# A heavier weight for the 47-point groups in the pace that mixes spectral steps into channel mixing

## The chip, the core and the metric

The kernel runs on one core of one Trainium2 chip. The metric is device microseconds of one execution, lower is better; what is compared is the median of several runs. A profiled execution has its own time, and inside it a span from the first to the last instruction.

## The reference

The input `x` is 8 batches of 3008 positions by 256 channels in float32. Two blocks follow one another.

```python
X = np.fft.rfft(x, axis=1)
Yr = Xr @ w_r - Xi @ w_i + b_r          # complex 256x256 mixing of channels
Yi = Xr @ w_i + Xi @ w_r + b_i
Yr = sign(Yr) * max(|Yr| - 0.01, 0)     # the same for Yi
x = np.fft.irfft(Yr + 1j * Yi, n=3008, axis=1)

h = max(x.T @ w_tok1, 0) @ w_tok2       # token mixing, 3008 -> 256 -> 3008
u = x + h.T
out = u + max(u @ w_ch1, 0) @ w_ch2     # channel mixing, 256 -> 1536 -> 256
```

## The kernel before

**The arithmetic.** Matrix products that need float32 accuracy are made from a high and a low part of each operand: `mm3` (lines 195 to 198) issues three matmuls, high by high, high by low and low by high. So most products stand in the profile as three groups, at L196, L197 and L198, and each operand costs a cast on ScalarE (L146) or a copy on VectorE (L148), and a subtraction at L149 on VectorE or GpSimd, that make its two parts (`split`).

**The two kinds of work.** The spectral side works on units: batch 0 (unit 0), batch 1 (unit 1), then the pairs of batches 2 and 3, 4 and 5, 6 and 7 (units 2, 3 and 4). For a unit it does two things in turn.

- The 47-point groups (`dft47`, lines 286 to 312, 13 of them per unit). A group loads a tile `x` of up to 480 KB on SyncE's DMA queue (L439), three groups ahead; forms sums and differences (`sum_diff`, tile `sd`: GpSimd adds at L247, VectorE subtracts at L248; for unit 1 VectorE does both); splits them into `xh` (ScalarE, L146) and `xl` (VectorE, L149); multiplies them on TensorE (`stage1`, six matmuls into the PSUM tiles `p`); evicts the products on ScalarE into `a` (L269); and stores `a` to DRAM on ScalarE's DMA queue (L271, tile `a_d`). The pool of `a` has two buffers, so the eviction of one group waits until the store of the group two before it has landed. Units 2, 3 and 4 have two batches: a matmul is 512 columns wide, and tile `a` is 480 KB. Unit 1 has half of that.
- The spectral steps (`spectral`, lines 556 to 599). A step is one of 12 pairs of frequencies for one batch: `forward` (eight small matmuls at L469 into `px`, evicted by ScalarE to `xf` at L471, summed by GpSimd at L472, split to `xth` on ScalarE and `xtl` on VectorE), then one step later `mix` (18 matmuls into `pm`, then bias and soft threshold on VectorE at L498 to L506, and a split `yh`, `yl` on ScalarE and GpSimd), then three or four steps later, once for all batches of the unit, `inverse` (`pi`, stored to DRAM as `b_d`) and `tokens` (`gp`).

The channel side (`channel`, lines 800 to 881) handles a chunk of up to 512 positions: 12 times `first` (six matmuls into `ph`; ScalarE makes `hh` at L814, VectorE makes `hlo` at L815) and `second` (six matmuls into `po`). Now and then it builds the input of the next chunk (`make_u`, tile `pu`), for which tiles `wt` of 940 KB and `b` of 480 KB are loaded on SyncE's queue.

**How the two are put together.** Channel mixing of a unit has spectral work of later units beside it (`BESIDE`, line 40): unit 1 beside the channel mixing of unit 0, unit 2 beside that of unit 1, units 3 and 4 beside that of unit 2. After about 1575 us there is channel mixing alone. `channel` and `spectral` are generators, which give back the TensorE time of what they have just issued, as a planned figure in microseconds: a chunk in pieces of 1.37 or 2.73, a `make_u` as 3.6; a group as 0.7 for one batch and 1.4 for two (line 312), a step as 0.9 for `forward`, 2.15 for `mix`, and per batch 0.68 for `inverse` and 1.37 for `tokens`. Per batch that is 13 times 0.7 and 12 times 5.1, or 70.3 (line 1054).

The loop at the end (lines 1045 to 1077) holds what is left: `left_s` of spectral work and `left_c` of channel work. The pace is `left_s / left_c`, and after each piece of the channel it issues spectral pieces until the two are in proportion again:

```python
while left_s > pace * left_c:
    step = next(sp, None)
    ...
    left_s -= step
```

Spectral work says `"wait"` twice per unit, before its first group (units 2 to 4, line 288) and between the groups and the steps (line 560). Then 10 units of channel work pass alone (`hold`), and the pace is worked out anew from what is left. Three groups of unit 1 are issued before the loop begins; what they count for is `done`.

The instructions of one engine run in the order of its own queue, which is close to the order of the program but not the same: where the program is built, matmuls of neighbouring pieces are interleaved.

Of the kernel before, what the change touches and what calls it, by code (L numbers as in the profile page):

```python
# [17 lines left out]
B, N, C = 8, 3008, 256  # L18
# [5 lines left out]
UNITS = [[0], [1]] + [[2 * p, 2 * p + 1] for p in range(1, NP)]  # L24
NG = 13
# [11 lines left out]
SEVEN = (3, 4)  # L37
SPILL = (3, 4)
CW7 = 2 * CW
BESIDE = {0: [1], 1: [2], 2: [3, 4]}  # L40


# [84 lines left out]
def tile_kernel(ctx: ExitStack, tc: tile.TileContext, io):  # L127
# [115 lines left out]
    def sum_diff(x, g, w, eng, pool):  # L243
        if eng is None:
            return x
        sd = t4([120, 2, w], "sd") if pool is None else wk.tile([120, 2, w], F32, tag=("xtl", "xf", "wt", "et")[g % 4], name="sd", bufs=2)
        eng.tensor_tensor(out=sd[:, 0], in0=x[:, 0], in1=x[:, 1], op=ALU.add)  # L247
        V.tensor_tensor(out=sd[:, 1], in0=x[:, 0], in1=x[:, 1], op=ALU.subtract)  # L248
        return sd

    def split_x(sd, w):
        xh, xl = hl([120, 2, w], "xh"), hl([120, 2, w], "xl")
        split(xh, xl, sd, S, V)
        return xh, xl

    def stage1(sd, dst, g, w, pool):
        n = GS if g < NG - 1 else N2 - GS * (NG - 1)
        a = ev([120, 2, w], "a") if pool is None else pool.tile([120, 2, w], F32, name="a", bufs=4)
        each = 512 // w
        for i0 in range(0, 2, each):  # L260
            pt = bank("p1")
            for i in range(i0, i0 + each):
                o = (i - i0) * w
                if pool is None:
                    mm3(pt[:, o:o + w], f1r[:, 0, i], f1r[:, 1, i], sd[0][:, i], sd[1][:, i], True, True)
                else:
                    PE.matmul(pt[:120, o:o + w], lhsT=f1[:, i], rhs=sd[:, 0], start=True, stop=False)
                    PE.matmul(pt[:120, o:o + w], lhsT=f1[:, 2 * i], rhs=sd[:, 1], start=False, stop=True)
            S.copy(out=a[:, i0:i0 + each].rearrange("p i w -> p (i w)"), in_=pt[:120])  # L269
        rows = dst.rearrange("(i n) k w -> (n k) i w", i=2)  # L270
        PUT.dma_start(out=rows[g * 120:g * 120 + n * KH, :, :w], in_=a[:n * KH])  # L271


    def stage1_turned(sd, z, g):
        n = GS if g < NG - 1 else N2 - GS * (NG - 1)
        pt = bank("p1")
        for t in range(2):
            for i in range(2):
                o = (2 * t + i) * GS * KH
                PE.matmul(pt[:, o:o + GS * KH], lhsT=sd[:, i, t * 128:(t + 1) * 128], rhs=f1[:, i], start=True, stop=True)  # L280
        S.copy(
            out=z.rearrange("p k (q n) -> p q k n", q=4)[:, :, :, g * GS:g * GS + n],
            in_=pt[:, :4 * GS * KH].rearrange("p (q n k) -> p q k n", q=4, n=GS)[:, :, :, :n],
        )

    def dft47(load, dst, w, ahead, eng, pool=None, turned=False):
        xs = [load(g) for g in range(ahead)]
        yield "wait" if eng is G else 0.0
        sds = {}

        def prepare(g):
            if g < NG:
                sds[g] = sum_diff(xs[g], g, w, eng, pool)
                xs[g] = None

        def divide(g):
            if g < NG and pool is None:
                sds[g] = split_x(sds[g], w)

        prepare(0)  # L300
        prepare(1)
        divide(0)
        for g in range(NG):
            if g + ahead < NG:
                xs.append(load(g + ahead))
            prepare(g + 2)
            divide(g + 1)
            if turned:
                stage1_turned(sds.pop(g), dst, g)
            else:  # L310
                stage1(sds.pop(g), dst, g, w, pool)
            yield 0.7 * w / C

    def f2cols(k1):
        j0 = (15 * k1) % N2
# [11 lines left out]
    def prepare_w1(pool, after):  # L327
        def load(g):
            f = load_wide(None, 2 * DT, pool, ("hl", "o")[g % 7 % 2], raw=raws.pop(g), after=after.get(g)).rearrange("p (i w) -> p i w", i=2)
            load_raw1()  # L330
            return f

        return dft47(load, a_w, DT, 2, None, pool)
# [222 lines left out]
    def spectral(u):  # L556
        p = parts(u)
        nb = p.nb
        yield from dft47(p.load_unit, p.a, p.w, 3, V if u == 1 else G)
        yield "wait"  # L560
        steps = [(kp, b) for kp in range(KP) for b in range(nb)]
# [42 lines left out]
    def begin(sp):  # L604
# [14 lines left out]
        with tc.tile_pool(name="early", bufs=1) as early:  # L619
# [3 lines left out]
            wc["fw"] = early.tile([128, 2, 128], F32, name="fw")  # L623
            z = wc["z"] = const.tile([128, KH, 2 * 128], F32, tag="w1", name="z")
            x = dft47(p.load_unit, z, p.w, NG, V, early, True)
            DMA.dma_start(out=wc["eye"], in_=io["eye"])
            next(x)
# [81 lines left out]
    for u, bs in enumerate(UNITS):  # L709
        total, at = N * len(bs), 0  # L710
        step = CW7 if u in SEVEN else CW
        widths = [k * TOKS for k in sizes] if u == 0 else [total % step] + [step] * (total // step)
# [47 lines left out]
    def make_u(g):  # L760
# [6 lines left out]
        for m in homes:  # L767
            if m not in ufs:
                ufs[m] = wc["uf"].tile([128, 2, CW7 if chunks[m][0] in SEVEN else CW], F32, name="uf", bufs=3)
        for ct in range(2):  # L770
# [230 lines left out]
    def channel7(ns):  # L1001
        channels.close()
        wc["tail"] = ctx.enter_context(tc.tile_pool(name="tail", bufs=1, reuse_waits="tile"))
        behind = None
        half = NF // 2
        for n in ns:
            after = n + 1 if n + 1 < len(chunks) else None
            mine = list(needs[after]) if after else []
            for p in range(half):
                hs = first7(n, p)  # L1010
                if behind:
                    second7(*behind, 0, (0, 1))
                if p < len(mine):
                    make_u(mine[p])
                    if p + 1 < len(mine):
                        load_wt2(mine[p + 1])
                        load_b2(mine[p + 1])
                if p == half - 2:
                    load_ahead(n + 2)
                if behind:  # L1020
                    second7(*behind, 1, (0, 1))
                    if p == 0:
                        for k in range(2):
                            finish7(behind[0], k, 2)
                behind = n, p, hs
                if after and p == half - 2:
                    sum_u(after)
                    for i in range(2):
                        split_u7(after, i)
                if after and p == half - 1:  # L1030
                    for i in range(2, 7):
                        split_u7(after, i)
        for k in range(2):
            for f in range(2):
                second7(*behind, f, (k,))
            finish7(behind[0], k, 2 - k)

    def run(gen):
        for _ in gen:
            pass  # L1040
# [3 lines left out]
    done = begin(sp)  # L1044
    for n, (u, at, cw) in enumerate(chunks):
        if u in SEVEN:
            channel7(range(n, len(chunks)))
            break
        if at == 0:
            if u:  # L1050
                sp, done = chain.from_iterable(spectral(v) for v in BESIDE[u]), 0.0
            else:
                sp = chain(sp, *(spectral(v) for v in BESIDE[u][1:]))
            left_s = sum(len(UNITS[v]) for v in BESIDE[u]) * 70.3 - done
            mine = [w for cu, _, w in chunks if cu == u]
            made = sum(k for gu, _, _, k in groups if gu == u) - sizes[0]
            left_c = 32.7 * (sum(mine) - mine[-1]) / CW + 3.6 * made * TOKS / GW + 0.5
            pace, hold = 0.0, left_c - (25.0 if u == 0 else 0.0)
        for c in channel(n):
            if c == "end":  # L1060
                run(sp)
                left_s = -1e9
                continue
            left_c -= c
            if hold is not None:
                if left_c > hold:
                    continue
                pace, hold = left_s / left_c, None
            while left_s > pace * left_c:
                step = next(sp, None)  # L1070
                if step is None:
                    left_s = -1e9
                elif step == "wait":
                    hold = left_c - 10.0
                    break
                else:
                    left_s -= step
# [36 lines left out]
```

## Time and profile before

| what | value |
|---|---|
| median of 3 runs | 2419.73 us (2414.97 to 2424.8) |
| time of the profiled execution | 2420.43 us |
| its span, first to last instruction | 2418.6 us |
| TensorE busy in the span | 2382.5 us |
| mean granted clock of TensorE in the span | 0.998 |
| channel mixing beside spectral work | about 150 to 1575 us |
| groups of unit 2, 3 and 4 on TensorE | 475 to 523, 846 to 893, 1213 to 1259 us |
| DMA traffic over the span | 250.29 MB, mean 103 GB/s |

Busy time of TensorE counts each matmul from its start to a modelled end, and these overlap; so a busy TensorE may still be a stalled one in part, but an idle one is surely waiting. The rows of a view by windows give a stretch of the span, its length, then for each engine its busy microseconds with the count of instructions, the granted clock of TensorE as a share of full speed, the mean busy share of the 16 DMA engines, and GB/s.

### The profile page before, as it was taken

The page shows a single profiled execution, that of the slowest core. Times are in us where ns is not written, and L with a number is a line of the kernel's source. Part 1 is how long each engine was busy: PE and PEld are TensorE (multiplying, and loading weights), DVE is VectorE, ACT ScalarE, POOL GpSimd, SP SyncE. Part 2 cuts the span into 40 slices and gives each one's busy share as a digit, 9 for nine tenths or more (in the row PEclk, how much of TensorE's full clock was granted, in tenths as well). Part 3 has the DMA queues.
Part 4 walks back from the last instruction along what each step waited for, and adds up shares of the span by engine and source line. Part 5 has one row for each costly group of instructions (what it writes and reads, how often), then busy time and mean ns, then how long its engine had stood idle before and what let it go on. Part 6 is the DMA issues. An engine that isn't in the chain of part 4 may idle for free.

```text
span 2418.6 us, 32117 instructions
## 1 busy us (share of the span) xinstructions
PE 2382.5 (99%) x12632; PEld 2077.9 (86%) x12632; DVE 1324.2 (55%) x2070; ACT 1080.3 (45%) x1931; POOL 307.2 (13%) x259
## 2 busy tenths in 40 slices
PE   8999999989999999999999999999999999999999
PEld 7878999978888878888878888898888889888887
DVE  7985655345444455454555544545555554555554
ACT  6764444243333253333353433345445444544543
POOL 0000222022222122222222222000000000000000
PEclk9999999999999999999999999999999999999999
DMA  8874344362323362323472231422221122222100
GB/s 209 249 221 146 96 123 143 107 200 90 93 89 93 102 210 75 117 79 104 129 226 92 88 97 45 134 72 60 72 64 48 42 66 81 59 72 64 48 1 35
DMA packets 145155, 250.29 MB, mean 103 GB/s; under 512 B 10421, under 2 KB 98317, under 8 KB 145005
## 3 DMA queue, kind: packets, MB, share of 16 engines
q1 hardware_dynamic: 114649, 192.67, 27.0%
q10 hardware_dynamic: 30356, 55.58, 7.1%
q8 instruction: 99, 1.62, 0.3%
q14 instruction: 51, 0.42, 0.1%
HBM read 161.84 MB, written 86.38 MB: 103 GB/s over the span
## 4 chain that ended last, share of the span: by engine, by line
PE 91%; DVE 3%; DMA 3%; ACT 1%; issue 1%; SPq 1%; POOL 0%; ACTq 0%; DVEq 0%; POOLq 0%
PE po L196 10%; PE po L198 10%; PE po L197 10%; PE ph L196 5%; PE ph L197 5%; PE ph L198 5%; PE pu L776 5%; PE px L469 3%; PE pm L196 2%; PE pm L198 2%; PE pm L197 2%; PE sx L196 2%; PE sx L198 2%; PE sx L197 2%; PE pu L196 2%; PE pu L197 2%
## 5 line engine op out<-in xcount | busy, mean ns | idle before, releaser
L196 PE MATMUL po<-hh,w2h 128*128 128x512 f32 (+4 forms) x1176 | 451.8, 384 | 0.0
L197 PE MATMUL po<-hlo,w2h 128*128 128x512 f32 (+4 forms) x1176 | 449.0, 382 | 0.0
L198 PE MATMUL po<-hh,w2l 128*128 128x512 f32 (+4 forms) x1176 | 448.8, 382 | 0.0
L815 DVE SCALAR_TENSOR_TENSOR hlo<-ph,hh 128x512 fp32r<-128x512 f32 (+4 forms) x300 | 196.5, 655 | 253.2 <-ACT hh L814 251.9
L814 ACT ACTIVATE hh<-ph 128x512 fp32r<-128x512 f32 (+4 forms) x300 | 171.7, 573 | 279.8 <-PE ph L198 271.5
L198 PEld LDWEIGHTS po<-hh,w2l 128*128 128x128 f32 x1176 | 221.1, 188 | 38.6
L197 PEld LDWEIGHTS po<-hlo,w2h 128*128 128x128 f32 x1176 | 221.2, 188 | 37.6 <-DVE hlo L815 0.5
L196 PEld LDWEIGHTS po<-hh,w2h 128*128 128x128 f32 x1176 | 221.3, 188 | 37.3
L196 PE MATMUL ph<-uh,w 128*128 128x512 f32 (+4 forms) x600 | 230.7, 385 | 6.3 <-ACT a L269 4.9
L197 PE MATMUL ph<-ul,w 128*128 128x512 f32 (+4 forms) x600 | 227.4, 379 | 0.0
L198 PE MATMUL ph<-uh,w 128*128 128x512 f32 (+4 forms) x600 | 226.8, 378 | 0.0
L944 ACT ACTIVATE hh<-sn 128x512 fp32r<-128x512 f32 (+1 forms) x288 | 180.5, 627 | 57.9 <-DVE sn L964 37.8
L945 DVE SCALAR_TENSOR_TENSOR hlo<-sn,hh 128x512 fp32r<-128x512 f32 (+1 forms) x288 | 193.5, 672 | 7.0 <-ACT hh L944 0.6
L149 DVE TENSOR_TENSOR xtl<-xf,xth 128x768 fp32r<-128x768 f32 x84 | 81.4, 969 | 139.6 <-ACT xth L146 139.6
L953 DVE TENSOR_TENSOR sn<-sq,sn 128x512 f32<-128x512 f32 (+1 forms) x72 | 48.9, 679 | 195.5 <-PE sq L198 181.0
L196 PE MATMUL pm<-wmh,xth 128*128 128x256 f32 x504 | 146.9, 292 | 2.8 <-ACT xth L146 2.8
L198 PE MATMUL pm<-wmh,xtl 128*128 128x256 f32 x504 | 142.3, 284 | 1.0 <-DVE xtl L149 1.0
L949 ACT COPY sn<-sx 128x512 f32<-128x512 f32 (+1 forms) x72 | 41.7, 579 | 227.5 <-PE sx L198 227.4
L197 PE MATMUL pm<-wml,xth 128*128 128x256 f32 x504 | 142.3, 283 | 0.0
L783 ACT COPY uf<-pu 128x470 f32<-128x470 f32 (+20 forms) x164 | 61.3, 407 | 179.2 <-PE pu L776 178.7
L776 PEld LDWEIGHTS pu<-g,b 96*128 96x128 f32 x1024 | 130.8, 191 | 3.4
L196 PEld LDWEIGHTS ph<-uh,w 128*128 128x128 f32 x600 | 113.0, 188 | 23.7 <-ACT a L269 6.4
(185 smaller groups left out, 4858.0 us busy)
## 6 DMA issues: line engine op xcount, KB each, us to landing
wt<-wt_d SPq DMA_DIRECT2D x28, 940.0 KB, 5.7
x<-in_x SPq DMA_DIRECT2D x39, 480.0 KB, 5.0
a<-a_d SPq DMA_DIRECT2D x36, 512.0 KB, 3.8
b_d<-bt ACTq DMA_DIRECT2D x36, 512.0 KB, 3.3
a_d<-a ACTq DMA_DIRECT2D x36, 480.0 KB, 4.7
wt<-wt_d SPq DMA_DIRECT2D x21, 752.0 KB, 4.9
b<-b_d SPq DMA_DIRECT2D x32, 480.0 KB, 6.3
aw<-w_d SPq DMA_DIRECT2D x48, 256.0 KB, 2.7
```

Source lines behind the costliest of these rows:

```text
L149: lo_eng.tensor_tensor(out=lo, in0=src, in1=hi.bitcast(F32), op=ALU.subtract)
L196: PE.matmul(out, lhsT=wh, rhs=xh, start=start, stop=False, skip_group_check=more)
L197: PE.matmul(out, lhsT=wh, rhs=xl, start=False, stop=False, skip_group_check=more)
L198: PE.matmul(out, lhsT=wl, rhs=xh, start=False, stop=stop, skip_group_check=more)
L469: PE.matmul(pt[:, o:o + 128], lhsT=x, rhs=f2cols(2 * kp + ab), start=True, stop=True)
L776: PE.matmul(pt[:, s * TOKS:(s + 1) * TOKS], lhsT=b2[:, s, cs], rhs=g2[:, 0 if s0 + s == 0 else 1], start=False, stop=s == k - 1)
L783: S.copy(out=ufs[m][:, ct, lo - at:hi - at], in_=pt[:, lo - c0:hi - c0])
L814: S.activation(out=hh, in_=pt, func=AF.Relu)
L815: V.scalar_tensor_tensor(out=hlo, in0=pt, scalar=0.0, in1=hh.bitcast(F32), op0=ALU.max, op1=ALU.subtract)
L944: S.activation(out=hh, in_=t, func=AF.Relu)
L945: V.scalar_tensor_tensor(out=hlo, in0=t, scalar=0.0, in1=hh.bitcast(F32), op0=ALU.max, op1=ALU.subtract)
L953: V.tensor_tensor(out=snap[0], in0=q, in1=snap[0], op=ALU.add)
```

## The change

A group beside channel mixing counts for 1.75 per batch in place of 0.7, in the figure that it gives back and in the sum that the pace is worked out from. `NG` is 13. No instruction is added, removed or altered in itself; the order in which the program issues them changes. The groups of the preparation that come with a pool of their own keep 0.7.

```diff
+SLOW = 1.75
 BESIDE = {0: [1], 1: [2], 2: [3, 4]}
...
-            yield 0.7 * w / C
+            yield (SLOW if pool is None else 0.7) * w / C
...
-            left_s = sum(len(UNITS[v]) for v in BESIDE[u]) * 70.3 - done
+            left_s = sum(len(UNITS[v]) * (70.3 + NG * (SLOW - 0.7)) for v in BESIDE[u]) - done
```

## The prediction

> **What bounds the kernel now.** I read the page first, for how much there is to win.
>
> ```profile
> span 2418.6 us, 32117 instructions
> PE 2382.5 (99%) x12632; PEld 2077.9 (86%) x12632; DVE 1324.2 (55%) x2070; ACT 1080.3 (45%) x1931; POOL 307.2 (13%) x259
> ```
>
> TensorE is busy for all but 36.1 us of the span, and the change takes no matmul away. So a gain can come only from those 36 us, and from time in which TensorE runs slowly. The next question is where they lie. I went through the span in windows of 25 us, and then asked for the stages that stood out: the groups of units 2, 3 and 4 (first three rows), those of unit 1 after them, a stretch of steps of units 2, 4 and 3, and channel mixing alone in the last row.
>
> ```profile
> core 0: us, PE busy (x) PEld busy (x) DVE busy (x) ACT busy (x) POOL busy (x), PEclk, DMA share, GB/s
> 475.00:525.00 50.00, 43.73 (x197) 35.99 (x196) 28.93 (x28) 28.54 (x47) 15.63 (x9) 0.93 0.80 239
> 845.00:895.00 50.00, 47.47 (x229) 39.55 (x228) 30.93 (x32) 30.35 (x50) 16.08 (x9) 1.00 0.71 215
> 1213.00:1263.00 50.00, 47.44 (x225) 38.49 (x225) 28.05 (x29) 30.09 (x49) 16.18 (x9) 1.00 0.78 232
> 185.00:210.00 25.00, 25.00 (x144) 22.60 (x143) 21.34 (x43) 16.52 (x31) 0.00 (x0) 1.00 0.67 196
> 575.00:725.00 150.00, 149.88 (x861) 132.22 (x861) 73.06 (x109) 58.98 (x103) 38.01 (x36) 1.00 0.29 91
> 1325.00:1475.00 150.00, 149.51 (x856) 132.04 (x855) 71.13 (x106) 57.83 (x103) 38.07 (x35) 1.00 0.29 91
> 950.00:1100.00 150.00, 149.51 (x848) 131.64 (x848) 67.21 (x100) 56.79 (x99) 33.12 (x31) 1.00 0.31 94
> ...
> 425.00:475.00 50.00, 50.00 (x283) 48.02 (x281) 17.11 (x27) 12.19 (x26) 3.18 (x2) 1.00 0.25 71
> ```
>
> The reader sees two regimes. In the steps TensorE idles 0.12 to 0.49 us in 150. In the groups of the three double units it idles 6.27, 2.53 and 2.56 us in 50, and in the first of them the granted clock is 0.93. In those rows DMA is at 215 to 239 GB/s, where the steps have 91 to 94. Unit 1's groups, half as large, idle nothing at 196 GB/s. Next, who TensorE waits for, over the whole span, and below it what ScalarE waits for between 470 and 530 us.
>
> ```profile
> PE p L197 <- DVE xl L149: 6.2, 7, 1.6
> PE ph L196 <- ACT a L269: 4.9, 3, 2.3
> PE pm L196 <- ACT xth L146: 2.8, 4, 1.1
> PE p L196 <- ACT a L269: 0.5, 1, 0.5
> PE pm L198 <- DVE xtl L149: 1.0, 2, 0.5
> ```
> ```profile
> ACT a L269 <- DMA a_d<-a: 10.7, 4, 5.5
> ```
>
> Columns are microseconds, times, longest. Eleven waits (6.2 + 4.9 + 0.5 us) belong to the groups. Where the releaser is ScalarE's eviction `a`, ScalarE itself stood up to 5.5 us for a store of an earlier group to land, and everything behind it in its queue stood too, the `hh` of channel mixing included. The DMA view of 475 to 525 us shows the crowd (issues, KB each, median us to landing):
>
> ```profile
> a_d<-a ACTq DMA_DIRECT2D x12, 480.0 KB, 5.0
> x<-in_x SPq DMA_DIRECT2D x6, 480.0 KB, 6.1
> wt<-wt_d SPq DMA_DIRECT2D x2, 940.0 KB, 7.7
> b<-b_d SPq DMA_DIRECT2D x2, 480.0 KB, 10.0
> ```
>
> **What the change does to the order.** I ran the loop by hand on its own planned figures. When the groups of unit 2 begin, `left_c` is 163.8 both before and after; `left_s` is 2 x 70.3 = 140.6 before and 2 x (70.3 + 13 x 1.05) = 167.9 after. The pace goes from 0.858 to 1.025. A group of two batches is paid with 1.4 / 0.858 = 1.63 us of channel work before and 3.5 / 1.025 = 3.41 us after; with its own 1.4 us it comes every 3.0 us, then every 4.8. The same for unit 3 (0.736 to 0.879): 3.3, then 5.4. Unit 4 (0.817 to 0.976): 3.1, then 5.0. Unit 1 (0.421 to 0.486, one batch): 2.4, then 4.3. Before, two or three groups of a double unit often stand together between two pieces of channel work; after, 3.5 exceeds what one piece of 2.73 pays for, and they stand singly. The steps pay for it. After their hold, unit 2 has 122.4 us of steps to place beside 129.8 of channel work before and 107.1 after: pace 0.943, then 1.143. Unit 1: 0.456, then 0.529; unit 3: 0.763, then 0.910; unit 4: 0.890, then 1.092. That is 16 to 23% closer. All steps still end before the channel mixing beside them does, so no flush at a unit's end is added, and the 845 us after 1575 us are untouched.
>
> **Groups: what goes.** First, idle time in the three rows: 6.27 + 2.53 + 2.56 = 11.4 us. Second, the clock: 7% of 50 us, 3.5 us. Third, what a wait costs beside its idle time:
>
> ```profile
> 508.66 0.40 PE L197 MATMUL p<-xl,f1r 120*128 120x512 f32 x1
> 508.90 0.39 PE L198 MATMUL p<-xh,f1r 120*128 120x512 f32 x1
> 511.58 0.47 PE L196 MATMUL ph<-uh,w 128*128 128x448 f32 x1 [2.29 <-ACT a L269]
> 511.89 0.36 PE L197 MATMUL ph<-ul,w 128*128 128x448 f32 x1
> ```
>
> In a row the next matmul starts 0.24 us after the one before, though that one lasts 0.40; idle time is counted from its end, so a wait hides 0.16 us more, and the first matmul after it takes 0.47 where its neighbour takes 0.36. That is some 0.25 us for each of ten such waits in these stages (one of the eleven I leave to the preparation): 2.5 us. Together 17.4 us could go.
>
> Would they go? In the 50 us of unit 2, 12 stores, 6 loads of `x`, 2 of `wt` and 2 of `b` were asked for. A unit has 13 stores and those 6 loads, 19 x 0.49 MB = 9.3 MB; beside channel work alone there are 71 GB/s. At one group in 3.0 us, 13 groups take 39 us and ask for 239 + 71 = 310 GB/s, which no window of the table shows; at 4.8, 5.4 and 5.0 us they take 62, 70 and 65 us and ask for 150, 133 and 143, with the 71 some 221, 204 and 214 GB/s. The nearest rows are unit 1 with 196 GB/s and no idle time, and unit 3 with 215 and 5%, which holds pairs and triples that the change takes apart. Each store may take two groups' distance to land, some 6.0 us before and 9.6 after, against a median of 5.0. So I let the even spacing remove most, and keep 2.5 us of waits (between 0, by unit 1's row, and 6, by 5% of 62 and 65 us), where a `wt` and a `b` land in the middle of a group.
>
> The clock term needs a look of its own, in windows of 2 us.
>
> ```profile
> 511.00:513.00 2.00, 1.42 (x6) 1.05 (x6) 0.50 (x2) 2.00 (x4) 0.00 (x0) 0.92 0.24 91
> 513.00:515.00 2.00, 1.54 (x4) 0.92 (x4) 1.97 (x3) 2.00 (x4) 0.70 (x1) 0.50 0.89 248
> ...
> 519.00:521.00 2.00, 0.76 (x3) 0.15 (x1) 1.95 (x2) 0.00 (x0) 0.00 (x0) 0.87 0.58 169
> ```
>
> The clock falls to half right after the longest wait of the stage, 2.29 us, which followed one of 1.29; I take it as their consequence, and as gone with them. Unit 4's stage had one wait of 1.8 us and kept its clock, which speaks a little against that:
>
> ```profile
> PE ph L196 <- ACT a L269: 1.8, 1, 1.8
> ```
>
> The Trainium skill, "TensorE: Matmul & The Clock Gate", Part 1: The HAM clock gate, has the clock halve after an idle window of about 3.4 us; no wait here is that long, so by that rule the fall has another cause, its 3.5 us would stay, and the sum below would be 2409.5. Here the clock fell without such a wait and directly behind the shorter ones, and the same 50 us are the only ones of the three rows with both.
>
> **Steps: what comes.** The chain from `forward` to `mix` is a sum of four rows of tile `xf`:
>
> ```profile
> L471 ACT COPY xf<-px x96: 566/587/595, 24.4 to 1507.9; 128x512 f32<-128x512 f32 x96
> L472 POOL TENSOR_TENSOR xf<-xf x84: 731/738/1541, 228.1 to 1508.7; 128x256 f32<-128x256 f32 x84
> L146 ACT CAST xth<-xf x84: 831/834/841, 229.5 to 1509.4; 128x768 fp32r<-128x768 f32 x84
> L149 DVE TENSOR_TENSOR xtl<-xf,xth x84: 948/959/1426, 230.4 to 1510.3; 128x768 fp32r<-128x768 f32 x84
> ```
>
> That is 3.1 us by the medians. By the planned figures the usual distance is 5 to 20 us before and after; distances of 3.1 us or less, the first step of each unit aside, are 2 before and 5 after (in unit 2 at its eighth and last step, in unit 3 at the third and eighteenth, in unit 4 at the last). The two waits `pm` <- `xtl` of 0.5 us are the price of one: 3 x 0.5 = 1.5 us more. Against it the first `mix` of unit 1 moves from 0.9 to 3.4 us behind its `forward`, and of unit 2 from 0.9 to 2.3; four such waits were 2.8 us, so some 1.0 us goes. Density as such: unit 2's row at pace 0.943 idles less than unit 3's at 0.763, so 1.143 is not far into a worse regime. VectorE is at 73.06 of 150 there, and 10% more leaves it at 54%. I add 0.5 us in all, with ends at -2 (first waits gone) and +6 (twelve tight steps more than I count).
>
> **The sum.** Against the profiled execution's own 2420.4 us: - 11.4 - 3.5 - 2.5 + 2.5 + 0.5 = - 14.4, so 2406.0 us. Its own time is 0.7 us above the median of 2419.73, so I take the same figure for the median. The ends: all waits gone and -2 give 2420.4 - 17.4 - 2 = 2401; 6 us of waits left, +6 in the steps, and the clock unchanged give 2420.4 - 17.4 + 6 + 6 + 3.5 = 2418.5.
>
> **The rivals.** (a) DMA stays the bound of a group and half of the 17.4 us remains: 2420.4 - 8.7 + 0.5 = 2412. For it speaks that a longer phase meets one more `wt` and `b`, and that 214 to 221 GB/s is the 215 at which unit 3 idled; against it the even spacing and the longer time for a store. 18%. (b) The clock's fall has a cause other than these waits and stays: 2406.0 + 3.5 = 2409.5. For it speak the 1.8 us of unit 4 that left its clock alone. 7%. This is what the Trainium skill's rule above would make of it. (c) The spacing is lost again where the matmuls are interleaved at build, which the trace shows for neighbouring pieces: groups as close as now, 2420. Only distances of a piece or so move there, so 6%. (d) Slower: `mix` of most steps finds its `xtl` late, because closer steps put `mix` right behind `forward`. The three double units and unit 1 have 84 steps; at 0.5 us each, 30 of them eat the 14.9 us that the groups give, and 54 make the kernel 12 us slower. At 60 it is 2420.4 - 14.9 + 30 = 2435.5. Before, two steps of 84 paid this and pace 0.943 shows none, so 5%.
>
> **How the numbers follow.** A difference of 0.5%, 12.1 us, is about what a measurement of this kernel can tell from no change; the three runs shown lie 9.8 us apart. So faster means below 2407.6. The forecast has 62%, of which some 9 points lie above that line, as 2406.0 is close to it. Rivals (a), (b) and (c) have 31% and all count as the same, (d) 5% slower, and 2% I leave for small losses elsewhere, as the same. That makes 0.53 faster, 0.42 same, 0.05 slower. The range goes from 2400, just under the lower end, to 2418: it takes in (a) and (b) and leaves out (c), (d) and the rest of the tails, some 17%.
>
> **What would show it.** Right: the first and last matmul of the groups of units 2, 3 and 4 lie 60 to 70 us apart; in that stretch TensorE idles under 1.5 us per unit; `ACT a <- DMA a_d` falls from 10.7 us in unit 2 to under 3; no window before the last few us has a clock under 1.00 after 150 us; the steps begin 15 to 25 us later and end where they did. Wrong: waits of `ph` on `a` or of `p` on `xl` that stay above 5 us in total (rival a); a clock at half speed somewhere in channel mixing without waits ahead of it (b); groups still 3 us apart (c); waits `pm` <- `xth` or `xtl` that grow past 10 us (d).

## The result and the profile after

The changed kernel takes 2402.32 us (median of 4 runs, 2400.64 to 2404.4) against 2418.8 us (4 runs, 2414.97 to 2424.8): 16.5 us less, a ratio of 0.993 with a 95% interval of 0.9907 to 0.9953. The forecast was 2406.0, some 14 us less, within 2400 to 2418. The two profiled executions lie 19.8 us apart (2420.43 and 2400.64).

The page of the changed kernel opens with the same work in a shorter span (line numbers are one higher from line 40 on):

```profile
span 2398.9 us, 32115 instructions
PE 2374.6 (99%) x12632; PEld 2076.2 (87%) x12632; DVE 1324.7 (55%) x2070; ACT 1079.2 (45%) x1931; POOL 306.6 (13%) x259
```

The windows view of the changed kernel, over its own groups of units 2, 3 and 4 (first three rows), and over stretches of steps of units 2 and 4:

```profile
472.00:532.00 60.00, 60.00 (x284) 51.35 (x283) 34.12 (x37) 34.19 (x56) 13.70 (x9) 1.00 0.68 205
835.00:904.00 69.00, 69.00 (x340) 59.65 (x339) 36.26 (x42) 35.91 (x61) 14.65 (x9) 1.00 0.61 177
1196.00:1260.00 64.00, 64.00 (x303) 53.63 (x302) 32.84 (x37) 34.33 (x56) 16.20 (x9) 1.00 0.66 193
560.00:710.00 150.00, 148.75 (x877) 131.99 (x876) 78.18 (x117) 61.38 (x107) 42.36 (x39) 1.00 0.31 94
1325.00:1475.00 150.00, 150.00 (x872) 133.07 (x871) 74.23 (x110) 60.07 (x106) 41.24 (x38) 1.00 0.29 91
```

The groups now take 60 to 69 us of the span in place of 47 or 48, and TensorE idles nothing in them, at a full clock. That is the 11.4 us of idle time and the 3.5 us of lost clock. What TensorE still waits for after 150 us lies all in the stretches of the steps:

```profile
PE pm L197 <- ACT xth L147: 2.5, 4, 0.9
PE pm L199 <- DVE xtl L150: 1.0, 2, 0.5
PE pi L197 <- DVE hlo L816: 0.8, 1, 0.8
PE po L198 <- DVE hlo L816: 0.4, 2, 0.2
```

No line of `p`, and none of `ph` on `a`, is left there. (A second profiled execution of the changed kernel, further below, has one such wait of `ph` on `a`, 0.6 us in unit 4.) Cutting both traces at 150 and 1575 us shows that the gain lies between; first before, then after:

```profile
150.00:1575.00 1425.00, 1407.17 (x7841) 1247.18 (x7842) 733.84 (x1092) 583.55 (x1028) 304.47 (x253) 1.00 0.39 117
```
```profile
150.00:1575.00 1425.00, 1419.85 (x7942) 1263.94 (x7941) 744.64 (x1107) 592.34 (x1045) 303.86 (x253) 1.00 0.39 118
```

Idle time there falls from 17.8 to 5.2 us, 12.7 us, and 101 more matmuls fit into the same 1425 us. Of the 17.8 us, 1.3 are the end of a wait for `gh` that began before 150 us and does not belong to the change; the section on the prediction comes back to it.

### The profile page after: what moved, and what is told of

Same layout as the page of the kernel before. It is cut to its first block, busy times and chain, and to the rows that moved or that the text cites. A ratio compares the mean times of both kernels' runs of the same rounds, so it can differ in the third digit from the quotient of the medians.

```text
span 2398.9 us, 32115 instructions
## 1 busy us (share of the span) xinstructions
PE 2374.6 (99%) x12632; PEld 2076.2 (87%) x12632; DVE 1324.7 (55%) x2070; ACT 1079.2 (45%) x1931; POOL 306.6 (13%) x259
## 4 chain that ended last, share of the span: by engine, by line
PE 92%; DVE 3%; DMA 2%; ACT 1%; POOL 1%; SPq 1%; issue 0%; ACTq 0%; DVEq 0%; POOLq 0%
PE po L198 11%; PE po L197 11%; PE po L199 11%; PE ph L197 5%; PE ph L198 5%; PE ph L199 5%; PE pu L777 5%; PE px L470 3%; PE pm L199 2%; PE pm L197 2%; PE pm L198 2%; PE sx L197 2%; PE sx L198 2%; PE sx L199 2%; PE pu L197 2%; PE pu L198 2%
## 5 line engine op out<-in xcount | busy, mean ns | idle before, releaser
L777 PE MATMUL pu<-g,b 96*128 96x94 f32 x1024 | 129.2, 271 | 0.0
```

The costliest lines, as they stand in the source:

```text
L777: PE.matmul(pt[:, s * TOKS:(s + 1) * TOKS], lhsT=b2[:, s, cs], rhs=g2[:, 0 if s0 + s == 0 else 1], start=False, stop=s == k - 1)
```

## The experiments

The theory to begin with was the prediction's: in a crowd of groups ScalarE stands behind the store of an earlier tile, and the distance between groups is what a store's landing is to be weighed against. The first four kernels ask which of the two movements pays, the groups' or the steps', and how much of it is needed. Where one sentence gives a time before, it is that of the kernel before on the same chip.

**Steps late and close, groups as before.** The kernel before, with a longer pause between the last group of a unit and its first step:

```diff
-        yield "wait"          # between groups and steps
+        yield "rest"
-                elif step == "wait":
-                    hold = left_c - 10.0
+                elif step in ("wait", "rest"):
+                    hold = left_c - (10.0 if step == "wait" else 34.0)
```

> The order of before for the groups (weight 0.7, pace 0.858 in unit 2, one group in 3.0 us), but 34 us of channel work in place of 10 between a unit's last group and its first step, so that the steps stand about where the change puts them: pace 1.143 in unit 2, 0.566, 0.824 and 1.244 in units 1, 3 and 4. Theory (the time came from the groups standing further apart; closer steps cost about 1 us): the waits of the groups stay, 8 us or more of TensorE's waits on a and xl, and the time is that of before, 2416 to 2422 us. Rival (the later, denser steps are what pays): 2401 to 2407 us. Rival (dense steps cost much, and the groups pay even more): over 2425 us.

Measured: 2431.18 us against 2419.53, ratio 1.0043 (1.0029 to 1.0058): slower, and outside the first two expectations. The time is that of the third (over 2425 us), but not for its reason: the steps' waits (`pm` on `xth` 2.2 us, `pm` on `xtl` 1.0) are about those of the changed kernel. Its waits view and its windows show the groups:

```profile
PE p L197 <- DVE xl L149: 9.2, 8, 2.0
...
PE ph L196 <- ACT a L269: 5.2, 2, 3.3
```
```profile
476.00:526.00 50.00, 44.31 (x205) 36.89 (x205) 28.82 (x30) 29.59 (x49) 16.14 (x9) 0.97 0.84 253
847.00:897.00 50.00, 46.19 (x222) 38.23 (x221) 31.02 (x32) 29.87 (x50) 16.05 (x9) 1.00 0.71 215
1229.00:1281.00 52.00, 45.30 (x184) 34.37 (x183) 30.19 (x29) 28.33 (x46) 16.16 (x9) 0.90 0.71 209
```

Unit 4's row is the new one: 6.7 us idle, and a clock of 0.90, which is 5.2 us of 52; before, it had 2.6 us of idle time and a full clock. By the loop on its planned figures, the late steps of unit 3 leave unit 4's groups a pace of 0.893 in place of 0.817, so a group in 2.97 us in place of 3.1. That most of the loss stands in this row is measured; that the last tenth of a microsecond is its cause is only worked out. The edit also goes further than its aim: the first `mix` of units 2, 3 and 4 comes 21, 23 and 50 us later than before, where the change moves it by 8, 5 and 6 us. Still, the rival that the steps' new place pays is out: with it the kernel loses, and units 2 and 3, whose groups keep their pace, go on idling 5.7 and 3.8 us.

**The pairs of batches alone.** Unit 1 keeps its weight:

```diff
-            yield (SLOW if pool is None else 0.7) * w / C
+            yield (SLOW if pool is None and w > C else 0.7) * w / C
...
-            left_s = sum(len(UNITS[v]) * (70.3 + NG * (SLOW - 0.7)) for v in BESIDE[u]) - done
+            left_s = sum(len(UNITS[v]) * (70.3 + NG * (SLOW - 0.7) * (len(UNITS[v]) > 1)) for v in BESIDE[u]) - done
```

> The change for units 2, 3 and 4 alone; unit 1, whose groups are half as large, keeps 0.7. Theory: unit 1's groups never stalled before, so their spacing is worth at most the one wait of 1.1 us at their first step: 2402 to 2405 us. Rival (unit 1 has a share in the gain, by bytes 1/7 of it or more): 2405 us or more.

Measured: 2405.68 us, ratio 0.9949 (0.9935 to 0.9964). Between 200 and 260 us TensorE waits 1.1 us for `xth` and 0.6 us for `hlo` at unit 1's first steps, as in the kernel before and unlike the changed one: these 1.7 us are unit 1's share as the trace shows it. The time lies just inside the rival's range (2405 us or more) and its interval overlaps that of the full change. The slowest run, 2411.38 us, is the profiled one: its clock stands at half from about 152 to 163 us, where channel mixing begins, which costs 5 us; the other three lie at 2405.3 to 2405.8. As the medians of the kernel before differ by up to 3.0 us from one set of runs to the next, the size of unit 1's share stays open.

**A third of the way, and further.** `SLOW = 1.05` and `SLOW = 2.8`.

> A weight of 1.05, a third of the way: one group in 3.7, 4.1 and 3.8 us in units 2, 3 and 4 (before 3.0, 3.3, 3.1; changed 4.8, 5.4, 5.0). A unit's 9.3 MB in 48 to 53 us beside 71 GB/s ask for 247 to 265 GB/s, below what 25 us of before reached (287) but above the 215 at which there was 5% idle. Theory (DMA crowd): between the two, waits of the groups of 2 to 6 us, 2405 to 2412 us. Rival (proportional to the weight): 2413 us. Rival (any loosening that separates groups is enough): 2401 to 2404 us.

> A weight of 2.8: one group in 6.1, 6.9 and 6.3 us, the steps at pace 1.35, 1.06 and 1.28 (unit 2, 3, 4). Theory: the groups have no wait left to lose at 1.75, and the steps have room (VectorE under 60%): 2401 to 2406 us, the same as the change within 4 us. Rival (closer steps begin to pay 0.5 us at most mixings): 2412 us or more, with waits pm on xth or xtl over 10 us.

Measured: 2405.71 us at 1.05, ratio 0.9948 (0.9933 to 0.9962), and 2401.87 us at 2.8, ratio 0.9927 (0.9913 to 0.9942). A third of the added weight gives five sixths of the gain; the time lies within the theory's range, at its lower end, and not in that of either rival. The windows over the groups of units 2, 3 and 4 at 1.05:

```profile
473.00:523.00 50.00, 49.00 (x235) 42.03 (x234) 29.75 (x32) 30.96 (x51) 15.58 (x9) 1.00 0.81 245
837.00:890.00 53.00, 51.32 (x249) 43.98 (x248) 31.05 (x35) 31.42 (x52) 15.64 (x9) 1.00 0.69 203
1200.00:1250.00 50.00, 48.55 (x231) 39.79 (x230) 28.60 (x30) 30.30 (x49) 16.06 (x9) 1.00 0.79 236
```

The reader should set the first row beside unit 2 before: the same 50 us, 245 GB/s in place of 239, and 1.0 us idle in place of 6.3. So the mean rate of DMA is not what decides. Nor is ScalarE's wait for the stores by itself: in unit 2 it still adds up to 8.6 us here (10.7 before), and in unit 4 of the changed kernel to 6.2 us (6.8 before) beside a TensorE that idles nothing. That such a wait costs TensorE where groups follow so closely that nothing else is left to do is the reading that fits these rows. At 2.8 the steps stand at a pace of up to 1.35, and TensorE waits 3.5 us there for `xth` and `xtl`, as after the change. The rival of steps that come too close (d) has no trace of itself up to that point.

**More room for the stores, without any spacing.** The kernel before, with two more buffers for `a`:

```diff
-        a = ev([120, 2, w], "a") if pool is None else ...
+        a = wk.tile([120, 2, w], F32, tag=("ev", "wt")[g % 2], name="a", bufs=2) if pool is None else ...
```

> The order of before (weight 0.7), but the groups' eviction tile a alternates between two pairs of buffers, the second pair being that of the steps' tile wt, which is idle during the groups: four buffers in place of two. An eviction then waits for the store four groups back, 12 us in place of 6, where the stores took a median of 5.0 us and 9.5 at most. Theory (ScalarE, stuck behind a store, holds up xh, hh and all behind them): its wait for a_d falls from 10.7 us in unit 2 to under 1, the waits ph on a vanish, those of p on xl fall to under 2 us, the clock stays up, and half or more of the gain of the change comes without any spacing: 2404 to 2412 us. Rival (the engines' own work bunches up: VectorE, ScalarE and GpSimd cannot follow one group in 3.0 us): p still waits for xl by 5 us or more, 2416 us or more. Rival (DMA's rate as such, 310 GB/s asked): the wait moves from the stores to the loads of x, 2414 us or more.

Measured: 2415.24 us (10 runs, 2407.6 to 2416.26) against 2419.02, ratio 0.9973 (0.9961 to 0.9986). By the median the theory's range (2404 to 2412 us) is missed, and waits for `xl` of over 5 us are what the rival of bunched engines named; no instruction of these groups waits for a load of `x`, so the rival of DMA's rate is out. The theory's mechanism is there, and it is a part only: no eviction `a` waits for a store any more, `ph` never waits for `a`, and yet by the medians 12 of 16 us are not won. The profiled execution took 2410.62 us, one of the faster four of the ten; in it the groups of the three units idle 6.1 us in place of 11.4, and the clock stands at half for 3.4 us in place of 6.8. So the part of the stores is a quarter by the medians, and about half by the profiles. TensorE still waits for `xl`, as the waits view has it:

```profile
PE p L197 <- DVE xl L149: 6.3, 7, 1.9
```

The timeline of this kernel shows how. Three groups stand together:

```profile
500.29 0.69 DVE L248 TENSOR_TENSOR sd<-x 120x512 f32<-120x512 f32 x1
500.33 1.79 POOL L247 TENSOR_TENSOR sd<-x 120x512 f32<-120x512 f32 x1 [6.33 <-DVE xl L149]
...
500.90 2.31 DVE L149 TENSOR_TENSOR xl<-sd,xh 120x1024 fp32r<-120x1024 f32 x1
...
503.24 0.69 DVE L248 TENSOR_TENSOR sd<-x 120x512 f32<-120x512 f32 x1
...
503.26 0.50 PE L197 MATMUL p<-xl,f1r 120*128 120x512 f32 x1 [0.65 <-DVE xl L149]
503.29 1.79 POOL L247 TENSOR_TENSOR sd<-x 120x512 f32<-120x512 f32 x1 [1.16 <-DVE xl L149]
...
503.85 2.31 DVE L149 TENSOR_TENSOR xl<-sd,xh 120x1024 fp32r<-120x1024 f32 x1
...
506.22 0.51 PE L197 MATMUL p<-xl,f1r 120*128 120x512 f32 x1 [1.29 <-DVE xl L149]
```

VectorE does nothing else here than a 0.69 us difference and a 2.31 us subtraction per group, back to back, 2.95 us a group; TensorE needs 1.4. The subtraction has a median of 1.23 us elsewhere and takes longer while GpSimd's sum runs, which in turn begins only when the last subtraction ends. The Trainium skill, "SBUF — State Buffer", Who interferes with whom, says that a VectorE instruction with two inputs in SBUF contends with a GpSimd instruction that reads it; the 2.31 us beside a sum and the 1.23 us alone agree.

**The same, with the sum on VectorE.** To part these two engines:

```diff
-        eng.tensor_tensor(out=sd[:, 0], in0=x[:, 0], in1=x[:, 1], op=ALU.add)
+        (V if pool is None else eng).tensor_tensor(out=sd[:, 0], in0=x[:, 0], in1=x[:, 1], op=ALU.add)
```

> The kernel with four buffers for a and the order of before, and the groups' sum goes from GpSimd to VectorE. With four buffers no eviction waited for a store any more, but TensorE still waited 6.3 us for xl, all in bunches of groups: there VectorE's subtraction xl took 2.31 us in place of 1.23 while GpSimd's next sum, 1.80 us, ran, and the next sum began only when xl ended, so that a bunch went at 0.69 + 2.31 = 3.0 us a group. On VectorE alone a group takes 0.69 + 0.69 + 1.23 = 2.6 us. Theory (second half of the cause: the alternation of VectorE and GpSimd within a bunch): xl always 1.23 us, TensorE's waits for xl 2 to 4 us in place of 6.3, the time 2408 to 2413 us (2415.2 with GpSimd). Rival (xl is late for ScalarE's or the loads' sake): waits for xl 5 us or more, 2414 us or more. Rival (VectorE becomes the bound): waits of ph or po for hlo over 3 us, 2416 us or more.

Measured: 2413.3 us (8 runs, 2409.52 to 2417.01) against 2421.83, ratio 0.9964 (0.9951 to 0.9976). Its view of `xl`, and TensorE's waits:

```profile
L149 DVE TENSOR_TENSOR xl<-sd,xh x52: 678/1218/1227, 135.3 to 1248.6; 120x1024 fp32r<-120x1024 f32 x39, 120x512 fp32r<-120x512 f32 x13
```
```profile
PE p L197 <- DVE xl L149: 3.9, 6, 1.8
PE p L196 <- ACT xh L146: 3.2, 1, 3.2
...
PE po L197 <- DVE hlo L815: 1.6, 1, 1.6
```

No subtraction takes over 1.23 us any more, and the waits for `xl` fall as expected. The time is just above the range of the theory (2408 to 2413 us) and below those of the rivals, and it is not to be told from its neighbour's: the two intervals overlap over most of their length. In the trace, unit 2's groups idle 4.4 us between 470 and 525 us, with GpSimd's sums 4.1: one wait of 1.6 us for `hlo` at 514 us is new there. The wait for `xh` is not one of the bunches; it lies at 149.5 us, in the first groups of unit 1. So the slow subtraction is real, but that it costs time by itself is not shown; one wait that moved from `xl` to `hlo` suggests that within a bunch easing one helper hands the wait to the next.

**Stores doubled.** The other way round: the changed kernel, with a second store of each `a` of the pairs, to a tile that nobody reads:

```diff
+        if pool is None and w > C:
+            again = a_x[g % 2].rearrange("(i n) k w -> (n k) i w", i=2)
+            PUT.dma_start(out=again[g * 120:g * 120 + n * KH, :, :w], in_=a[:n * KH])
```

> The change, with each tile a of units 2, 3 and 4 stored twice, the second time to a tile that nobody reads: 6.4 MB more per unit, no other work added but the issue of 13 more DMAs. A unit asks for 15.7 MB in 62, 70 and 65 us, beside 71 GB/s: 295 to 324 GB/s, above the 287 that 25 us of before reached. Theory (the groups were held by the landing of their stores): the waits come back, ScalarE waits for a_d by 10 us or more per unit, and the time is 2410 to 2422 us. Rival (the engines' bunching was the cause, and it is gone): no change beyond 2 us, 2401 to 2404 us.

> The same doubled stores with a weight of 2.8: one group in 6.1, 6.9 and 6.3 us, so 15.7 MB in 80 to 90 us beside 71 GB/s, 245 to 267 GB/s, and 12 us for a store. Theory: the distance between groups is what a store's landing is to be weighed against, so the waits mostly go again: 2402 to 2408 us, and at least 5 us below the kernel with doubled stores at 1.75. Rival (doubled stores cost by themselves, by ScalarE's issue time or by DMA share): as slow as at 1.75.

Measured: 2411.12 us at 1.75, ratio 0.9967 (0.9955 to 0.9979), some 9 us above the changed kernel, with TensorE's wait for `a` back; and 2402.83 us at 2.8, ratio 0.9938 (0.9922 to 0.9953), the changed kernel's time again. At 1.75 ScalarE's waits for the landing of stores add up to 17.7 us (9.2 in the changed kernel), less than the 10 us per unit that were expected. What TensorE waits for most in its groups, and the windows over the three units:

```profile
PE p L197 <- ACT a L271: 4.3, 3, 1.6
```
```profile
472.00:538.00 66.00, 63.34 (x298) 53.34 (x297) 33.14 (x37) 34.06 (x56) 15.52 (x9) 1.00 0.85 272
839.00:908.00 69.00, 69.00 (x340) 59.63 (x339) 36.36 (x42) 36.06 (x62) 15.15 (x9) 1.00 0.80 256
1200.00:1268.00 68.00, 65.33 (x302) 52.85 (x301) 34.01 (x37) 33.39 (x55) 16.20 (x9) 1.00 0.83 268
```

So the stores' mechanism is real. Unit 3's row has 256 GB/s and no idle time, the other two 272 and 268 GB/s and 2.7 us each; as unit 3's groups also stand furthest apart (one in 5.4 us, against 4.8 and 5.0), the rows do not say whether the rate or the distance decides. The changed kernel has 177 to 205 GB/s in its rows.

**A version that goes further.** What is left in the changed kernel sits at tight places of the steps. The first `forward` of a unit gets a larger planned figure, so that its first `mix` stands further behind:

```diff
-                yield 0.9
+                yield 0.9 if n else 3.0
...
-            left_s = sum(len(UNITS[v]) * (70.3 + NG * (SLOW - 0.7)) for v in BESIDE[u]) - done
+            left_s = sum(len(UNITS[v]) * (70.3 + NG * (SLOW - 0.7)) + 2.1 for v in BESIDE[u]) - done
```

> The change, and the first forward of each unit counts for 3.0 in place of 0.9 (the sum for the pace has 2.1 more per unit), so that more channel work stands between it and the first mix: distances of 5.9, 5.0, 7.1 and 2.3 us by the planned figures in place of 3.4, 2.3, 0.9 and 0.9. What is left of waits after 150 us in the changed kernel is 5.2 us, of which four waits of pm on xth are 2.5. Theory: some 1 to 2 us of these go, 2400 to 2402 us, hardly to be told from the change. Rival (the order shifts and other tight places come up): 2403 to 2405 us.

Measured: 2398.25 us, ratio 0.9915 (0.9898 to 0.9931), more than expected. So both kernels ran once more on one chip:

> The changed kernel once more, on the chip of its neighbours in this list: 2400 to 2405 us.

> The change with the first forward of a unit counted as 3.0, once more, beside the changed kernel on one chip: 2397 to 2402 us, and 2 to 5 us below the changed kernel if the first look holds; within 1 us of it if that was scatter.

Measured: 2402.7 us for the changed kernel, ratio 0.9927 (0.9909 to 0.9946), and 2397.6 us for the one with its first steps apart, ratio 0.9901 (0.9886 to 0.9917), both against 2421.83. Both pairs of medians are 4 to 5 us apart, though the two intervals of the second pair overlap a little. Idle time between 150 and 1575 us is 2.7 us, where the changed kernel beside it has 5.7:

```profile
150.00:1575.00 1425.00, 1422.28 (x7949) 1267.09 (x7949) 746.10 (x1113) 592.35 (x1047) 302.29 (x253) 1.00 0.39 119
```

Only 0.6 of these 3.0 us are waits of a first `mix` (0.3 us each in units 3 and 4), which is what the edit aims at. The others went because the order shifted, and the remaining 1 to 2 us between the medians are not explained by idle time.

## Why the prediction was right, and where its steps were not

**What bounds it, and the sum.** The place was right: idle time and clock in the groups of units 2, 3 and 4. Between the profiled executions, the stages' 11.4 us of idle time and 3.5 us of clock went in full; the 2.5 us of waits kept for a `wt` and a `b` in the middle of a group did not come, as the three rows have none. That is the term that was mis-sized most: it was read from before's 215 GB/s, which held bunches, though the prediction itself said so.

What else lies between the two executions shows when both are counted from one matmul, the first that builds the input of a chunk from `gh`; first before, then after:

```profile
151.31 0.48 PE L196 MATMUL pu<-wt,gh 128*128 128x470 f32 x1 [1.69 <-ACT gh L547]
```
```profile
148.73 0.48 PE L197 MATMUL pu<-wt,gh 128*128 128x470 f32 x1 [1.21 <-ACT gh L548]
```

Up to there both kernels issue the same matmuls in the same order, so these 2.6 us are what two executions differ by. Behind it lie 17.1 of the 19.7 us between the spans. Idle time and clock are 14.9 of them, and the 2.5 us for the restarts, which no run measures, would make it 17.4.

**The steps' term** was 0.5 us of cost. From that matmul to 1575 us TensorE idles 16.5 us before and 5.2 after, and without the groups' 11.4 us it is 5.2 in both: the steps cost nothing. Two larger terms cancel in this. Of the five tight places that the prediction names, four came as waits, in unit 2 at the eighth and the last step, in unit 3 at the eighteenth, in unit 4 at the last:

```profile
608.54 0.39 PE L199 MATMUL pm<-wmh,xtl 128*128 128x256 f32 x1 [0.49 <-DVE xtl L150]
...
764.58 0.39 PE L197 MATMUL pm<-wmh,xth 128*128 128x256 f32 x1 [0.93 <-ACT xth L147]
...
1097.03 0.38 PE L199 MATMUL pm<-wmh,xtl 128*128 128x256 f32 x1 [0.49 <-DVE xtl L150]
...
1496.66 0.39 PE L197 MATMUL pm<-wmh,xth 128*128 128x256 f32 x1 [0.93 <-ACT xth L147]
```

That is 2.8 us, where before two places cost 0.5 us each: 1.9 us more, and 1.5 were forecast. Against it the waits of the first `mix` of each unit fell from 2.8 to 0.6 us, by 2.2 and not by 1.0: those of units 1 and 2 went, as listed, and unit 3's fell from 1.1 to 0.3 us, which nobody had named. Waits for `hlo` are 1.2 us before and after, at other places.

**The order** came out nearly as worked out: the matmuls of the groups lie 59, 68 and 63 us apart (62, 70 and 65). They do not all stand singly; four pairs that the loop had parted still start 1.5 us apart (one each in units 2 and 3, two in unit 4), as rival (c) has it, but TensorE does not idle at them. The steps begin only 6 to 8 us later, not 15 to 25, and their last `forward` comes 6 to 14 us earlier, not where it did: the removed stalls bring all that follows forward, and I had left them out there. ScalarE's wait for `a_d` in unit 2 fell from 10.7 to 2.2 us, as named.

**The cause** was right in part. The prediction took the landing of stores as what holds a group. Four buffers take that wait away and bring 4 of the 16 us by the medians and about half by the profiles; doubled stores bring it back and cost 9. The rest, half or more, belongs to groups standing in twos and threes: there TensorE's 1.4 us were shorter than what VectorE with GpSimd took (2.95 us). The weight of 1.05, which separates most groups at nearly the same GB/s, shows this best. How much of the gain belongs to each helper is open. The number came out even so because the sum takes the rows' idle time whole, whichever helper was late. That spacing would also cure the waits that no store causes was hardly argued in the prediction, and in that it had luck.

**The rivals.** (a), DMA as the bound of a group, is out at this spacing, as no wait is left in the rows. (b), a clock that falls for another reason, is out for this place, as the clock stayed at 1.00 in every row of the groups after; in the kernels that kept the bunches (before, steps late, four buffers with either engine) a fall stands in a row of the groups. The Trainium skill, "TensorE: Matmul & The Clock Gate", Part 1: The HAM clock gate, has the clock fall after an idle window of about 3.4 us. The trace does not agree: these falls came behind waits of 1.8 to 3.3 us at the longest. (c) is out by the groups' spans, but for the four pairs. (d) is out up to a pace of 1.35.

## What to carry to other kernels

Where one engine is full and others feed it, look at how the order bunches the pieces that load the others most: a planner that weighs pieces by the full engine's time alone will put them back to back. Here a heavier weight cost the full engine nothing, and a part of the way already gave most of the gain: the three weights tried, 1.05, 1.75 and 2.8, lie around 1.5 per batch, which is half of the 2.95 us that the slowest helpers took for a group of two. Two more buffers removed one kind of wait and left those of the other helpers, so an even order was the safer cure.

## What the runs showed of the hardware

- The granted clock fell to half without a long wait. With four buffers, the waits ahead of the fall were 1.9 us at the most, in bunched groups where TensorE was busy 3.47 and 3.15 of 5 us (first two rows); behind them the clock stood at 0.50 (third row), for 3.4 us in all:

```profile
505.00:510.00 5.00, 3.47 (x15) 2.68 (x16) 4.93 (x5) 3.56 (x6) 2.67 (x3) 1.00 0.98 336
510.00:515.00 5.00, 3.15 (x15) 2.40 (x14) 3.53 (x4) 2.27 (x5) 1.01 (x1) 1.00 0.86 274
```
```profile
516.00:519.00 3.00, 3.00 (x9) 2.32 (x8) 0.00 (x0) 1.17 (x2) 0.00 (x0) 0.50 0.45 101
```

- The scatter of the runs goes with it. The ten runs of this one kernel go from 2407.6 us at a mean clock of 0.999 to 2416.26 at 0.996; the changed kernel, whose clock was 0.999 or 1.0 in each of the four runs of the result, stays within 3.8 us; of its six later runs one fell to 0.997 and took 2411.5 us, the others 2402.1 to 2403.1. Such a fall needs no bunch of the pairs: the profiled runs of the kernel with unit 1 at its old weight and of the one with its first steps apart (both times) have one between 148 and 163 us, where channel mixing begins.
- A subtraction on VectorE of 120 by 1024 took 2.31 us beside a sum on GpSimd, and 1.23 us alone.
